# Three networks in one kernel: tiles moved to other start addresses, instructions unchanged

## The chip, the cores and the metric

The kernel runs on one core of a Trainium2 chip. The metric is the time of one execution on the device, in microseconds (us). The engines of the core are TensorE (PE, matrix products out of SBUF into PSUM), VectorE (DVE), ScalarE (ACT), GpSimd (POOL) and SyncE (SP, which issues loads and stores).

## The reference: what is computed

An attention with a sliding window and a few sink keys, then two feed-forward networks one after the other, all in float32:

```python
scores = np.where(keep, scale * (q @ k.T), -1e9)      # 2 x 8 heads x 768 x 64; keep: sink | window of 128
x = softmax(scores) @ v                               # as 1536 tokens x 512
h = x @ w_in                                          # 512 x 2048
g = where(h >= 1, h, where(h <= -1, 0, (h + 1)**2 / 4))
x = g @ w_out                                         # 2048 x 512
h = x @ w2_in
g = where(h > 0, h, exp(min(h, 0)) - 1)
out = g @ w2_out
```

The weights come as 64-bit floats and are turned into 32-bit ones on the chip.

## The kernel before

**Tiling.** Tokens lie on the free axis in three blocks of 512 (xh, xl: 128 partitions x 4 parts of the model width x 512 tokens). Each network takes the hidden width in 16 slices of 128. An item is one network, one block of 512 tokens, one slice: 2 x 3 x 16 = 96 items. For accuracy each operand of a product is split into a high part and the rest of it (xh and xl, wh and wl, gh and gl, written as fp32r by the copies and subtractions in lines 159, 161, 188 and 189), and each product is three matmuls: high x high, high x rest, rest x high.

**An item.** `gemm1` (line 172) makes h of 128 x 512 in 4 x 3 matmuls: the split first weights wh0, wl0 are stationary, the tokens xh, xl move, 512 columns in each. ScalarE and VectorE turn h into g and split it (lines 179 to 189). `gemm2` (line 211) adds the slice's part of the output to four PSUM tiles y0 to y3, again in 4 x 3 matmuls of 512 columns. In the first network the second weights wh1, wl1 are stationary and gh, gl move; in the second network gh, gl are stationary and wh1, wl1 move. The names in the trace don't carry the digit: wh in line 172 is wh0, in line 211 wh1. `finish` (line 268) does the second product of the last two items.

**Order.** `run` goes through the items: `gemm1` of item i, then `gemm2` of item i - 2. PE has this order written out, and so has GpSimd; the other engines have theirs from the program's order. In the first network `between` pulls in steps of attention: transposes of k and q with the identity idn moving (line 472), scores (509), transposes of the exponentials P, idn moving again (541), values (565), and the sinks' part, with pst moving (598, 602). Loads are issued by SyncE, some ahead of their use; conversion of the weights (lines 139 to 146) runs some units ahead of the items. There is a second path for other windows, behind a test at the end; it isn't taken here.

**Where tiles lie.** A pool takes the next free bytes of each partition, in the order in which pools are opened; a tile's start is rounded up to 32 bytes. `const` is first and holds small tiles, some of them asked for late. Then come the tokens (pool x), attention's pools (ld, v, qk, p, pt, xb, s), and the pools of `Moe` (wf, wst, wc, wsp, wso, mt, mg). nb, the row maxima of attention (asked for in line 498), is in attention's pool s.

Of the kernel before, what the change touches and what calls it, by code (L numbers as in the profile page):

```python
# [7 lines left out]
F32 = mybir.dt.float32  # L8
# [12 lines left out]
KW = BLK + NSINK  # L21
HB = BLK // 2
BW = KW + HB + NSINK
NEG = -1.0e30
FILL = -1.0e9


def f32(ap):
    return ap.bitcast(F32)


def read_params(nc, const, n_sink, window):
# [250 lines left out]
class Attn:  # L283


    def __init__(self, tc, ctx, q, k, v, xts, idn, const, segs, nq=2):
        self.tc, self.nc = tc, tc.nc
        nc = self.nc
        self.q, self.k, self.v, self.xts = q, k, v, xts
        self.B, self.H, self.S, self.D = q.shape  # L290
        self.scale = 1.0 / float(self.D) ** 0.5
        self.idn, self.const = idn, const
        self.nq = nq
        pool = lambda n, b, **kw: ctx.enter_context(tc.tile_pool(name="a_" + n, bufs=b, **kw))
        self.ld_p = pool("ld", 4)
        self.v_p = pool("v", 3)
        self.qk_p = pool("qk", 2)
        self.p_p = pool("p", 3)
        self.pt_p = pool("pt", 2)
        self.xb_p = pool("xb", 1)  # L300
        self.s_p = pool("s", 2)
        self.ps = pool("ps", 2, space=PSUM)
        self.sk, self.kept = {}, {}
        self.turn, self.spare = 0, []
        self.nat = {}
        self.first = None
        self.jobs = [(s, pr) for s in segs for pr in range(self.H // 2)]
        for what in "kq":
            self.load(what, *self.jobs[0])
# [8 lines left out]
    def masks(self, prm):  # L318
# [20 lines left out]
        for m, d, k in ((m0, far, ks), (m1, ring, kn)):  # L339
# [3 lines left out]
            nc.vector.tensor_scalar(out=m[:, sink], in0=key[:, 0:NSINK], scalar1=ns, scalar2=None, op0=ALU.is_ge)  # L343
            nc.vector.tensor_scalar(out=m, in0=m, scalar1=NEG, scalar2=None, op0=ALU.mult)
        nc.vector.tensor_scalar(out=m2[:, at], in0=ring, scalar1=w, scalar2=NEG, op0=ALU.is_ge, op1=ALU.mult)
        nc.vector.tensor_copy(m2[:, sink], m1[:, sink])
# [142 lines left out]
    def st_S(self, seg, pr, st):  # L489

        nc, D, nq = self.nc, self.D, self.nq
        b, q0 = seg[0], seg[1]
        qT, T = st["qk", pr]
        Tk = T.rearrange("p j k -> p (j k)")
        if "sm" not in st:
            st["sm"] = self.s_p.tile([128, nq, self.H], F32, tag="sm", name="sm")
            st["ps"] = self.s_p.tile([128, nq, self.H * (NSINK + 2)], F32, tag="psn", name="psn")
        nb = self.s_p.tile([128, nq, 2], F32, tag="nb", name="nb")
        P = st["P", pr] = self.p_p.tile([128, nq, 2, KW], F32, tag="P", name="P")
        S = [self.bank([128, 512], "S") for _ in range(2)]  # L500
        lead = HB + NSINK
        for n in range(nq):
            u = lead + n * BW
            for h in range(2):
                hs = slice(h * D, (h + 1) * D)
                for c in range(2):
                    o, r = (u - c * lead, n * KW + c * HB) if q0 + n else (u, KW)
                    N = (KW + (HB, lead)[c]) if q0 + n else KW
                    nc.tensor.matmul(S[h][c * HB:(c + 1) * HB, o:o + N], lhsT=qT[hs, n, c * HB:(c + 1) * HB],  # L509
                                     rhs=Tk[hs, r:r + N], start=True, stop=True, skip_group_check=True)  # L510
        n0 = 0 if q0 else 1
        for h in range(2):
            a = S[h][:, lead:lead + nq * BW].rearrange("p (n c) -> p n c", c=BW)
            lo = S[h][:, 0:nq * BW].rearrange("p (n c) -> p n c", c=BW)
            for c, to, data in ((0, a[:, :, 0:HB], a[:, :, KW:KW + HB]), (1, a[:, :, HB:BLK], lo[:, :, 0:HB])):
                r = slice(c * HB, (c + 1) * HB)
                nc.vector.copy_predicated(to[r, n0:], self.pick[r].unsqueeze(1).to_broadcast([HB, nq - n0, HB]), data[r, n0:])
            for n in range(nq):
                o = P[:, n, h, :]
                dv = nc.vector.tensor_tensor_reduce(out=o, in0=a[:, n, 0:KW], in1=self.mask[min(q0 + n, 2)], op0=ALU.add, op1=ALU.min,  # L520
                                                    scale=-self.scale, scalar=3.0e38, accum_out=nb[:, n, h:h + 1])
                ac = nc.scalar.activation(o, o, AF.Exp, bias=nb[:, n, h:h + 1], scale=-1.0,  # L522
                                          accum_out=st["sm"][:, n, 2 * pr + h:2 * pr + h + 1])
        if (seg, pr) == self.jobs[2]:
            self.first = (ac.ins, dv.ins)
# [181 lines left out]
def attention_moe_moe(ctx, tc, q, k, v, n_sink, window, w_in, w_out, w2_in, w2_out, out):  # L707
    nc = tc.nc
    B, H, S, D = q.shape
    NT, DM = out.shape  # L710
    const = ctx.enter_context(tc.tile_pool(name="const", bufs=1))
    xp = ctx.enter_context(tc.tile_pool(name="x", bufs=1))
    ws = ((w_in, w_out), (w2_in, w2_out))

# [5 lines left out]
    nc.gpsimd.affine_select(out=idn, in_=idn, pattern=[[-1, 128]], compare_op=ALU.not_equal, fill=1.0, base=0,  # L720
                            channel_multiplier=1)
    NX = NT // 512
    xts = []
    for t in range(NX):
        xts.append((xp.tile([128, DM // 128, 512], F32R, tag=f"xh{t}", name=f"xh{t}"),
                    xp.tile([128, DM // 128, 512], F32R, tag=f"xl{t}", name=f"xl{t}")))
    full = [(t, 0, 512) for t in range(NX)]

    with ExitStack() as c2:
        NQ = 2  # L730
        segs = []
        for b in range(B):
            for q0 in range(0, S // BLK, NQ):
                tok = b * S + q0 * BLK
                segs.append((b, q0, tok // 512, tok % 512))
        attn = Attn(tc, c2, q, k, v, xts, idn, const, segs, nq=NQ)
        moe = Moe(tc, c2, ws, out, xts, (full, full), half)

        attn.load("q", *attn.jobs[1])
        warm = const.tile([128, 1], F32, tag="warm", name="warm")  # L740
        nc.scalar.activation(warm, half, AF.Exp)

        zero = moe.t_p.tile([128, 512], F32, tag="g", name="zero")
        nc.vector.memset(zero, 0.0)
        bank = moe.h_ps.tile([128, 512], F32, tag="h", name="warmup")
        for _ in range(3):
            nc.tensor.matmul(bank, lhsT=zero[:, 0:128], rhs=zero, start=True, stop=True)
        prm = params(nc, const, raw)
        attn.masks(prm)
        gen = attn.stages()  # L750
        done = [0]

        def go(n=None, upto=None):

            while done[0] < len(segs) and (n is None or n > 0) and (upto is None or done[0] < upto):
                if next(gen) is not None:
                    done[0] += 1
                n = None if n is None else n - 1

        need = [(t * 512 + c0 + n) // (NQ * BLK) for t, c0, n in full] + [0]  # L760
        attn.spare = [lambda shape, name, t=t: moe.y_ps.tile(shape, F32, tag=t, name=name) for t in ("y0", "y1", "y2", "y3")]
        attn.spare += [lambda shape, name: moe.h_ps.tile(shape, F32, tag="h", name=name)] * 2

        for what, j in (("k", 1), ("k", 2), ("q", 2), ("k", 3), ("q", 3), ("v", 0)):
            attn.load(what, *attn.jobs[j])
        attn.load_vsink()
        attn.sink_sets()
        with tc.manual_schedule(engines={mybir.EngineType.PE, mybir.EngineType.Pool}):
            moe.load(1)
            attn.load("v", *attn.jobs[1])  # L770
            moe.load(3)
            go(n=18)
            flag = windowed(tc, const, prm)
            go(upto=need[0])
        moe.behind = attn.first
        attn.spare = []
        credit = [0.0]

        def between(i):
            m, tb, f = moe.items[i]  # L780
            if m == 1 or done[0] >= len(segs):
                return
            j = i // moe.KF
            credit[0] += PULLS[j]
            while credit[0] >= 1.0:
                credit[0] -= 1.0
                if done[0] < len(segs):
                    go(n=1)
            if f == moe.KF - 1 and moe.last_call:
                go(upto=need[j + 1])  # L790

        moe.run(between)
# [40 lines left out]
```

## Time and profile before

| what | us |
|---|---|
| median of three runs | 667.52 |
| the three runs | 667.35, 667.52, 668.36 |
| the profiled execution | 668.36 |
| its span, first to last instruction | 666.2 |
| PE / ACT / DVE / POOL busy in it | 631.7 / 444.2 / 386.8 / 303.7 |

The profiled execution is one of the three. Busy time of PE is the union of matmuls whose ends are modelled and which overlap: one matmul stands with 0.39 us in the trace where the next begins 0.23 us later. So the pace of PE is read from the distance of starts, or from the chain of waits, and not from the time of one matmul. The granted clock is the share of TensorE's full clock (2.4 GHz) in a stretch.

### The profile page before, as it was taken

Reading aid. Unit: us, or ns where it says so; the run is one execution under the profiler, and the core shown is the slowest. Engines: PE = TensorE matmul, PEld = TensorE weight load, DVE = VectorE, ACT = ScalarE, POOL = GpSimd, SP = SyncE. Lnnn points to the kernel's source line nnn. Section 1 sums busy time; section 2 is a strip of 40 time slices with the busy share of each in tenths; the row PEclk is TensorE's granted clock in tenths of the full one; section 3 lists DMA queues with packets and bytes.
Section 4 is the critical chain, followed back from the end, with each engine's and each line's share of the span. In section 5 each row is a group of like instructions: output and inputs, shape, how many; then the busy total and the mean of one; then the engine's idle time right before and its main releaser. Section 6 shows DMA issues by size and latency. Waiting matters only on the chain.

```text
span 666.2 us, 9583 instructions
## 1 busy us (share of the span) xinstructions
PE 631.7 (95%) x3202; PEld 489.3 (73%) x3202; DVE 386.8 (58%) x805; ACT 444.2 (67%) x922; POOL 303.7 (46%) x337
## 2 busy tenths in 40 slices
PE   6678989989999999999999999999999999999996
PEld 3446766756767777788788888888888888888884
DVE  5689999999736443425988778776432222322221
ACT  5677989788667666657688777776655555555542
POOL 4462122522354555644546555555444444444431
PEclk9798999989999999999999999999999999999999
DMA  5666455456310100001534323330010000100001
GB/s 122 161 166 191 133 171 163 139 155 175 95 29 14 24 5 9 1 0 32 157 96 125 97 95 95 95 95 32 0 64 1 1 1 0 64 0 1 1 0 69
DMA packets 66923, 47.92 MB, mean 72 GB/s; under 512 B 44848, under 2 KB 61232, under 8 KB 66864
## 3 DMA queue, kind: packets, MB, share of 16 engines
q1 hardware_dynamic: 65632, 46.96, 24.6%
q8 instruction: 27, 0.44, 0.3%
q10 hardware_dynamic: 1232, 0.26, 0.2%
q14 instruction: 32, 0.26, 0.1%
HBM read 44.06 MB, written 3.15 MB: 71 GB/s over the span
## 4 chain that ended last, share of the span: by engine, by line
PE 75%; DVE 8%; ACT 6%; DMA 4%; issue 3%; POOL 1%; SPq 1%; POOLq 0%; ACTq 0%; DVEq 0%
PE h L172 34%; PE y L211 33%; PE ops L565 2%; PE S L509 2%; DMA st<-in_moe_w_in_dram 2%; DVE ca L144 2%; DVE F L146 2%; ACT P L522 1%; PE qkps L472 1%; PE tps L541 1%; ACT F L140 1%; ACT ca L139 1%; DMA kn<-in_k_dram 1%; DVE ca L143 1%; PE y L268 1%
## 5 line engine op out<-in xcount | busy, mean ns | idle before, releaser
L161 POOL TENSOR_TENSOR wl<-F,wh 128x512 fp32r<-128x512 f32 x160 | 219.8, 1378 | 220.7 <-ACT wh L159 204.8
L159 ACT CAST wh<-F 128x512 fp32r<-128x512 f32 x192 | 117.0, 617 | 97.5 <-PE h L172 87.5
L172 PE MATMUL h<-xh,wh 128*128 128x512 f32 x384 | 154.3, 402 | 0.8 <-DVE g L181 0.5
L172 PE MATMUL h<-xl,wh 128*128 128x512 f32 x384 | 152.3, 397 | 0.9 <-POOL xl L609 0.9
L172 PE MATMUL h<-xh,wl 128*128 128x512 f32 x384 | 151.9, 395 | 0.0
L189 DVE TENSOR_TENSOR gl<-g,gh 128x512 fp32r<-128x512 f32 x96 | 72.7, 758 | 51.5 <-ACT gh L188 51.1
L185 DVE SCALAR_TENSOR_TENSOR g<-g,h 128x512 f32<-128x512 f32 x48 | 33.0, 687 | 115.4 <-ACT g L184 115.4
L188 ACT CAST gh<-g 128x512 fp32r<-128x512 f32 x96 | 59.6, 621 | 57.1 <-DVE g L185 36.1
L172 PEld LDWEIGHTS h<-xh,wh 128*128 128x128 f32 x384 | 72.0, 188 | 21.3 <-issue 3.6
L172 PEld LDWEIGHTS h<-xl,wh 128*128 128x128 f32 x384 | 72.2, 188 | 18.3 <-POOL xl L609 1.5
L172 PEld LDWEIGHTS h<-xh,wl 128*128 128x128 f32 x384 | 72.1, 188 | 17.3
L211 PE MATMUL y<-gh,wh 128*128 128x512 f32 x192 | 77.9, 406 | 0.0
L146 DVE CUSTOM_DVE_ANT_0 F<-ca,F 128x1024 uint16<-128x1024 uint16 x64 | 74.3, 1164 | 4.3 <-DVE ca L144 1.8
L211 PE MATMUL y<-gl,wh 128*128 128x512 f32 x192 | 75.4, 393 | 0.0
L211 PE MATMUL y<-gh,wl 128*128 128x512 f32 x192 | 75.4, 393 | 0.0
L211 PE MATMUL y<-wl,gh 128*128 128x512 f32 x184 | 72.1, 392 | 0.0
L211 PE MATMUL y<-wh,gh 128*128 128x512 f32 x184 | 71.8, 390 | 0.0
L211 PE MATMUL y<-wh,gl 128*128 128x512 f32 x184 | 71.6, 389 | 0.0
L181 DVE SCALAR_TENSOR_TENSOR g<-h,g 128x512 f32<-128x512 f32 x48 | 32.9, 686 | 52.0 <-ACT g L180 51.6
L547 POOL TENSOR_SCALAR_AFFINE_SELECT pt<-pt 128x512 f32<-128x512 f32 x48 | 35.7, 744 | 32.5 <-ACT pt L545 30.9
L139 ACT ACTIVATE ca<-st 128x512 f32<-128x512 f32 x64 | 43.1, 674 | 7.4 <-DVE F L146 3.4
L144 DVE SCALAR_TENSOR_TENSOR ca<-st,ca 128x512 int32<-128x512 int32 x64 | 47.3, 742 | 1.1
(111 smaller groups left out, 887.9 us busy)
## 6 DMA issues: line engine op xcount, KB each, us to landing
st<-in_moe_w_in_dram SPq DMA_DIRECT2D x32, 512.0 KB, 3.9
st<-in_moe_w_out_dram SPq DMA_DIRECT2D x32, 512.0 KB, 3.5
kn<-in_k_dram SPq DMA_DIRECT2D x48, 64.0 KB, 2.1
vn<-in_v_dram SPq DMA_DIRECT2D x32, 96.0 KB, 2.3
out_dram<-o SPq DMA_DIRECT2D x12, 256.0 KB, 2.1
qn<-in_q_dram SPq DMA_DIRECT2D x44, 64.0 KB, 2.1
vn<-in_v_dram SPq DMA_DIRECT2D x16, 64.0 KB, 3.3
qn<-in_q_dram ACTq DMA_DIRECT2D x4, 64.0 KB, 4.0
```

The lines of the kernel that those rows point to most:

```text
L139: nc.scalar.activation(a, w1.bitcast(F32), AF.Copy, scale=2.0 ** -112)
L144: nc.vector.scalar_tensor_tensor(out=ai, in0=w1, scalar=-0x80000000, in1=ai, op0=ALU.bitwise_and, op1=ALU.bitwise_or)
L146: nc.vector.tensor_tensor(out=r, in0=ai, in1=r, op=ALU.add)
L159: nc.scalar.copy(hi, src)
L161: (nc.vector if i < self.KF else nc.gpsimd).tensor_tensor(out=lo, in0=src, in1=f32(hi), op=ALU.subtract)
L172: nc.tensor.matmul(h, lhsT=w[:, k * 128:(k + 1) * 128], rhs=x[:, k, c0:c0 + n], start=(k == 0 and p == 0), stop=(k == self.KD - 1 and p == 2))
L181: nc.vector.scalar_tensor_tensor(out=g, in0=h, scalar=1.0, in1=g, op0=ALU.max, op1=ALU.min)
L185: nc.vector.scalar_tensor_tensor(out=g, in0=g, scalar=-1.0, in1=h, op0=ALU.add, op1=ALU.max)
L188: ac = nc.scalar.copy(gh, g)
L189: dv = nc.vector.tensor_tensor(out=gl, in0=g, in1=f32(gh), op=ALU.subtract)
L211: nc.tensor.matmul(self.y[c], lhsT=a, rhs=b, start=(first and p == 0), stop=(last and p == 2))
L547: nc.gpsimd.affine_select(out=o, in_=new, pattern=[[0, 2 * nq], [-sg, 128]], compare_op=op, fill=0.0, base=0, channel_multiplier=sg)
```

## The change

Three things are done to the pools. A tile that nothing writes, 32 bytes of it by `fill_to_row`, is put at the end of attention's pools, so that what comes next starts at a multiple of 256 bytes. The same is done at the end of `const`. And nb gets a pool of its own (a_nb, two buffers) behind `const`, ahead of the tokens. `CONST_END` and `ATTN_BYTES` are the bytes in use at those places. Each engine's instructions, their order, their operands apart from the addresses, and their waits are those of before.

```diff
--- before.py
+++ after.py
@@ -21,12 +21,21 @@
 KW = BLK + NSINK
 HB = BLK // 2
 BW = KW + HB + NSINK
+ROW = 256
+CONST_END = 26528 + 64
+ATTN_BYTES = 38656
 NEG = -1.0e30
 FILL = -1.0e9
 
 
 def f32(ap):
     return ap.bitcast(F32)
+
+
+def fill_to_row(pool, used):
+    n = -used % ROW
+    if n:
+        pool.tile([128, n // 4], F32, tag="fill", name="fill")
 
 
 def read_params(nc, const, n_sink, window):
@@ -300,6 +309,7 @@
         self.xb_p = pool("xb", 1)
         self.s_p = pool("s", 2)
         self.ps = pool("ps", 2, space=PSUM)
+        fill_to_row(pool("fill", 1), ATTN_BYTES)
         self.sk, self.kept = {}, {}
         self.turn, self.spare = 0, []
         self.nat = {}
@@ -495,7 +505,7 @@
         if "sm" not in st:
             st["sm"] = self.s_p.tile([128, nq, self.H], F32, tag="sm", name="sm")
             st["ps"] = self.s_p.tile([128, nq, self.H * (NSINK + 2)], F32, tag="psn", name="psn")
-        nb = self.s_p.tile([128, nq, 2], F32, tag="nb", name="nb")
+        nb = self.nb_p.tile([128, nq, 2], F32, tag="nb", name="nb")
         P = st["P", pr] = self.p_p.tile([128, nq, 2, KW], F32, tag="P", name="P")
         S = [self.bank([128, 512], "S") for _ in range(2)]
         lead = HB + NSINK
@@ -709,6 +719,7 @@
     B, H, S, D = q.shape
     NT, DM = out.shape
     const = ctx.enter_context(tc.tile_pool(name="const", bufs=1))
+    nb_p = ctx.enter_context(tc.tile_pool(name="a_nb", bufs=2))
     xp = ctx.enter_context(tc.tile_pool(name="x", bufs=1))
     ws = ((w_in, w_out), (w2_in, w2_out))
 
@@ -720,6 +731,7 @@
     nc.gpsimd.affine_select(out=idn, in_=idn, pattern=[[-1, 128]], compare_op=ALU.not_equal, fill=1.0, base=0,
                             channel_multiplier=1)
     NX = NT // 512
+    fill_to_row(const, CONST_END)
     xts = []
     for t in range(NX):
         xts.append((xp.tile([128, DM // 128, 512], F32R, tag=f"xh{t}", name=f"xh{t}"),
@@ -734,6 +746,7 @@
                 tok = b * S + q0 * BLK
                 segs.append((b, q0, tok // 512, tok % 512))
         attn = Attn(tc, c2, q, k, v, xts, idn, const, segs, nq=NQ)
+        attn.nb_p = nb_p
         moe = Moe(tc, c2, ws, out, xts, (full, full), half)
 
         attn.load("q", *attn.jobs[1])
```

Where tiles start within 256 bytes of a partition, from the built programs (several values are those of several buffers):

| tile | role | before | after |
|---|---|---|---|
| xh, xl | moving in line 172 | 160 | 0 |
| wh0, wl0 | stationary in line 172 | 224 | 0 |
| gh, gl | moving, then stationary in line 211 | 224 | 0 |
| wh1, wl1 | stationary, then moving in line 211 | 224 | 0 |
| st, F, ca, g | weights as loaded and converted, gate | 224 | 0 |
| kn, qn, vn | attention's loads | 160 | 0 |
| idn | moving in transposes | 192 | 192 |
| qkT | transposed k and q | 160, 0 | 0, 96 |
| P | exponentials | 96, 160, 224 | 192, 0, 64 |
| pt, pst, xb | transposed P, sinks, attention's output | 32 | 128 |
| vs, one | stationary beside pst | 160 | 192 |

Slices of 128 or 512 columns within these tiles lie at multiples of 512 bytes from their starts.

## Rows read from the trace of the kernel before

**Rows 1.** The page, part 1: engine, busy us, share of the span, instructions.
```profile
PE 631.7 (95%) x3202; PEld 489.3 (73%) x3202; DVE 386.8 (58%) x805; ACT 444.2 (67%) x922; POOL 303.7 (46%) x337
```

**Rows 2.** Busy us of each engine by stage, (x) instructions, granted clock, DMA share.
```profile
core 0: us, PE busy (x) PEld busy (x) DVE busy (x) ACT busy (x) POOL busy (x), PEclk, DMA share, GB/s
0.00:60.00 60.00, 41.84 (x348) 26.43 (x348) 41.85 (x172) 41.93 (x128) 32.07 (x90) 0.89 0.63 156
60.00:166.00 106.00, 97.87 (x556) 71.45 (x556) 100.01 (x242) 90.40 (x208) 27.75 (x45) 0.98 0.55 158
166.00:276.40 110.40, 108.91 (x646) 81.52 (x645) 55.91 (x146) 72.21 (x171) 55.92 (x67) 1.00 0.11 28
276.40:648.10 371.70, 371.46 (x1610) 301.22 (x1609) 185.57 (x244) 235.24 (x411) 185.41 (x135) 1.00 0.15 47
```

**Rows 3.** The chain that ended last, us 490 to 512: start, us, what.
```profile
498.69 2.80 PE h L172 x12
501.49 2.74 PE y L211 x12
```

**Rows 4.** PE's matmuls by line, from 276.4, from 166 and from 60 us.
```profile
L172 PE MATMUL h<-xh,wh 128*128 128x512 f32 x268 | 105.7, 394 | 0.2 <-DVE g L181 0.2
...
L211 PE MATMUL y<-wl,gh 128*128 128x512 f32 x180 | 70.6, 392 | 0.0
...
L211 PE MATMUL y<-gl,wh 128*128 128x512 f32 x88 | 34.5, 392 | 0.0
...
L211 PE MATMUL y<-gh,wh 128*128 128x512 f32 x58 | 24.2, 418 | 0.0
L172 PE MATMUL h<-xh,wh 128*128 128x512 f32 x57 | 24.0, 421 | 0.0
...
L172 PE MATMUL h<-xh,wh 128*128 128x512 f32 x55 | 23.0, 419 | 0.3 <-DVE g L181 0.3
...
L211 PE MATMUL y<-gh,wh 128*128 128x512 f32 x47 | 19.8, 421 | 0.0
```

**Rows 5.** PE's waits before 60 us: us in total, times, longest.
```profile
PE qkps L472 <- DMA kn<-in_k_dram: 6.8, 1, 6.8
PE tps L541 <- ACT P L522: 4.3, 5, 1.8
```

**Rows 6.** PE in order of time, one pass: start us, us, what.
```profile
498.53 0.39 PE L172 MATMUL h<-xh,wh 128*128 128x512 f32 x1
...
501.33 0.39 PE L211 MATMUL y<-wh,gh 128*128 128x512 f32 x1
...
502.71 0.39 PE L211 MATMUL y<-wh,gh 128*128 128x512 f32 x1
...
504.07 0.39 PE L172 MATMUL h<-xh,wh 128*128 128x512 f32 x1
```

**Rows 7.** The weight loads in the same pass (same columns).
```profile
498.54 0.19 PEld L172 LDWEIGHTS h<-xl,wh 128*128 128x128 f32 x1
...
501.33 0.19 PEld L211 LDWEIGHTS y<-wl,gh 128*128 128x128 f32 x1
```

**Rows 8.** PE in attention, from 34.7 us: start us, us, what, count.
```profile
34.81 0.38 PE L472 MATMUL qkps<-idn,kn 128*128 128x128 f32 x2
35.03 0.38 PE L472 MATMUL qkps<-idn,qn 128*128 128x128 f32 x2
...
38.32 0.40 PE L602 MATMUL rps<-pst,one 112*128 112x256 f32 x2
38.56 0.40 PE L598 MATMUL xps<-pst,vs 112*128 112x256 f32 x2
38.79 0.40 PE L602 MATMUL rps<-pst,one 112*128 112x256 f32 x2
```

**Rows 9.** ScalarE in the same pass as rows 6.
```profile
501.88 0.59 ACT L183 ACTIVATE g<-h 128x512 f32<-128x512 f32 x1
```

**Rows 10.** The page, part 6: issues, KB each, median us to landing.
```profile
kn<-in_k_dram SPq DMA_DIRECT2D x48, 64.0 KB, 2.1
```

## The prediction

> **What bounds the kernel now.** I read the busy line first: TensorE (PE) is busy for 631.7 of 666.2 us, no other engine for more than 444.2 [rows 1]. Such a share is a mean, so I cut the span into stages. From 276.4 to 648.1 us PE is busy for 371.46 of 371.70 us, at a granted clock of 1.00 (the 2.4 GHz level), while VectorE, ScalarE and GpSimd have 186, 235 and 185 us of work [rows 2]. The chain of waits says the same: 12 matmuls of line 172, then 12 of line 211, without end and with no other engine between them, 2.80 and 2.74 us each [rows 3]. Line 172 multiplies the tokens (moving xh, xl) by the split first weights, line 211 the gated part by the second weights. One pass of 24 matmuls takes 2.80 + 2.74 = 5.54 us, and there are 67 of them: three groups of 268 matmuls of line 172 in that stage, and of line 211 three of 180 (second network) and three of 88 (first), the first of each in [rows 4].
>
> Before that, PE is busy for 108.91 of 110.40 us from 166 to 276.4, and nearly all of it is on the chain again. From 60 to 166 us PE has 97.87 of 106 us and VectorE 100.01: VectorE bounds as much as PE. Before 60 us neither does alone (41.8 us each) [rows 2]; there PE waits 6.8 us for a load of k and 4.3 us for ScalarE's exponentials [rows 5].
>
> **The pace of one matmul.** Twelve matmuls of line 172 in 2.80 us are 233.3 ns each. The last six of a line 211 block go from 502.71 to the next block at 504.07: 1.36 us, 226.7 ns each; its first six take 1.38 us [rows 6]. A matmul of 512 columns at one column a cycle of 2.4 GHz is 512 / 2.4 = 213.3 ns. So a matmul of line 172 loses 20.0 ns and one of line 211 13.4 ns, though shape, type, clock and number of instructions are the same, and nobody is waited for. What differs? The moving operand of line 172 starts at byte 160 of a 256-byte row; that of line 211 at byte 224, in the first network (gh, gl) as in the second (wh1, wl1). The stationary operand starts at 224 in both lines. Its load cannot make the difference either: it begins within 0.01 us of the matmul before and takes 0.19 us in both lines [rows 6, 7]. So I read the two paces as the price of where the moving operand starts.
>
> What an operand at the start of a 256-byte row costs, this trace does not show for this kind of matmul. Bounds: below, 213.3 ns, which the clock sets; above, the 226.7 and 233.3 ns of today. The nearest row with a moving operand at a multiple of 64 bytes is that of the transposes: idn, at 192, moves in them. Two take 0.22 us, 110 ns each for 128 columns, which is two cycles a column (106.7 ns) and some 3 ns [rows 8]. They read at half the rate and so may hide a loss, but they show that little is lost between two matmuls as such. The products with pst moving (256 columns, start at 32) are the counter-case at full rate: 0.23 and 0.24 us for two, 115 to 120 ns where the clock allows 106.7, a loss of 8 to 13 ns on half as many columns, much like line 172's [rows 8]. I take 213.3 + 3 = 216 ns, the value nearest to the transposes.
>
> The Trainium skill (TensorE: Matmul & The Clock Gate, section "Wait — 56ns, not 53.3ns?") gives 215.7 ns from start to start for 512 columns at the full clock, without a word on where operands start. No matmul of 512 columns here reaches that; by it the sum below would be 30.4 us instead of 29.7.
>
> **The change part by part.** No instruction is added, taken away or moved, no wait and no DMA; the fillers are never written. What changes is where tiles start.
>
> Tokens, split weights and gated parts go from 160 and 224 to 0. A pass of 24 becomes 24 x 216 = 5.184 us. I leave the 0.02 us by which the first six of a line 211 block are slower (ScalarE reads h out of PSUM from 501.88 to 502.47 [rows 9]), so 5.204: 0.336 us gained per pass, 14.0 ns a matmul. Stage by stage:
> - 276.4 to 648.1 us: 67 passes x 0.336 = 22.5 us, all on the path. Who would be late next? The busiest other engine, ScalarE, has 235 us for what would be 349 [rows 2].
> - 166 to 276.4 us: 169 matmuls of line 172 (57 + 56 + 56) and 174 of line 211 (3 x 58; the first group of each in [rows 4]), 343 x 14.0 = 4.8 us, on the path since PE idles 1.5 us there.
> - 60 to 166 us: 167 (55 + 56 + 56) and 139 (47 + 46 + 46) = 306 matmuls [rows 4], 4.3 us. VectorE has only 6 us of slack there, and part of it is spent waiting for PE; I take half, 2.1 us, and keep nothing and 4.3 as ends.
> - after 648.1 us: 24 matmuls of line 268 (two last parts x 4 column blocks x 3), 0.3 us.
> Sum 29.7 us.
>
> Loads (kn, qn, vn, st) land at 0 instead of 160 or 224. Before 60 us this could touch the wait of 6.8 us for kn; from nothing to 6.8 either way. I take nothing: kn's median landing is 2.1 us [rows 10], so that wait is a queue of loads, not the slowness of one.
>
> Attention's own tiles only swap odd starts for odd starts: qkT from 160 and 0 to 0 and 96, P from 96, 160, 224 to 192, 0, 64, pt and pst from 32 to 128. Their matmuls are 250 + 303 = 553 in the two middle stages (556 - 306 and 646 - 343 [rows 2, 4]); most are fp32 products, which read no faster than the transposes. Nothing, with 553 x 3 ns = 1.7 us as the end either way. VectorE, ScalarE and GpSimd work on the same tiles; if their instructions change, they have a third of the long stage or more to hide it in [rows 2].
>
> Profiled run 668.4 - 29.7 = 638.7 us; the median of the three runs is 0.8 us under the profiled one, so 638 us.
>
> **The rivals.**
> *Part of the loss is not the start's.* The 13.4 ns of line 211 may be the price of changing stationary operands, with only the 6.7 ns between the lines due to the start (or to moving and stationary operand starting differently: 160 against 224 in line 172, 224 against 224 in line 211; after the change they agree everywhere). Then line 172 falls to 226.7 and line 211 stays: 6.7 ns x (804 + 169 + half of 167) = 7.1 us, 660 us. For: line 211's two halves of a network, with other operands moving, have one and the same loss. Against: the transposes change their stationary operand each time too and lose 3 ns. Between this and the forecast lies all from 645 to 664.
>
> *Starts do nothing.* The two paces could belong to something else that differs between the lines, such as 12 matmuls into one PSUM bank against 3. Against: inside its three, line 211 still goes at 226.7. Time: 667.5.
>
> The Trainium skill (SBUF — State Buffer, section "Specifications (TRN2)") speaks against this change: it counts in lines of 16 bytes, and 160, 224 and 0 are all multiples of 16, so by it all paces would be alike and the time would stay. Rows 6 disagree: 233.3 against 226.7 ns.
>
> *The row's start is the worst place: slower.* Two points allow another line: the pace falls by 6.7 ns as the start rises by 64 bytes, and jumps back at the block's end. With blocks of 128 bytes, 160 and 224 are 32 and 96, and 0 gives 236.7 ns: 12 x 3.3 + 12 x 10 = 160 ns more per pass, 10.7 us in the long stage and some 3.3 before, 681 us. With blocks of 256 bytes it gives 250 ns: 0.46 us a pass, 708 us. For: pst at 32 pays what 160 pays, as blocks of 128 say. Against: with blocks of 256 pst should take 123 ns, and it takes 115 to 120; and nothing in a read that begins at a boundary explains more work than one that straddles it. It decides as soon as the common pace is over 230.8 ns.
>
> **How the numbers follow.** Forecast (628 to 645 us): 0.55. Part of the loss only (645 to 664): 0.22. No change: 0.10. Slower: 0.13. The low end is the clock's: 17.5 ns x 2,281 matmuls = 39.9 us, 628. To leave out no more than 2 in 10 the range must take in no change: 628 to 668. A measurement can tell some 0.2% (1.3 us): faster 0.77, same 0.10, slower 0.13.
>
> **What would show it.** Right: in the long stage both lines' matmuls start 0.216 us apart, the chain's pieces of 12 are 2.60 us each and a pass 5.20 us, with the same counts of instructions. If line 172 alone falls to 0.227, the first rival holds; if both stay at 2.80 and 2.74, the second; if both stand at one pace over 0.231, the third. If the long stage gains 22 us and the stretch from 60 to 166 us nothing, VectorE took it. It is wrong if the gain lies before 60 us, in loads.

## The result, and the profile after

The changed kernel takes 662.06 us (median of 4 runs, 659.93 to 662.74) against 667.94 us for the kernel before (4 runs, 667.35 to 668.46). The ratio is 0.9907, with a 95% interval of 0.9882 to 0.9931: faster by some 0.9%, 5.9 us. The forecast was 638 us. A second set of runs of the same kernel (e7 below) gave 0.988 (0.9852 to 0.9908). The sign was right; the size was a fifth of what was forecast, and the time is that of the first rival.

One thing is not as the section on the change has it. `fill_to_row` puts 32 bytes behind `const`, but nothing behind attention's pools: without nb they take 38,656 bytes, which is already a multiple of 256. So what brought the networks' pools to 0 is that nb left attention's pools.

The profiled execution took 662.16 us, its span is 660.0 us. First the page's busy line, to be held against [rows 1], then the stages (columns as in [rows 2]), then the chain of waits as in [rows 3]. Line 181 is now the first product (172 before), line 220 the second (211 before).

```profile
PE 623.8 (95%) x3202; PEld 489.7 (74%) x3202; DVE 386.0 (58%) x805; ACT 445.1 (67%) x922; POOL 305.1 (46%) x337
```

```profile
60.80:168.30 107.50, 97.77 (x563) 72.05 (x564) 102.08 (x246) 92.56 (x212) 27.79 (x46) 1.00 0.56 159
168.30:276.20 107.90, 106.69 (x639) 80.27 (x638) 53.68 (x143) 70.95 (x169) 56.98 (x67) 1.00 0.10 26
276.20:641.70 365.50, 365.03 (x1610) 301.62 (x1609) 185.53 (x244) 235.47 (x411) 186.22 (x135) 1.00 0.15 48
```

```profile
495.03 2.72 PE h L181 x12
497.75 2.72 PE y L220 x12
```

The same 1610 matmuls of the long stage take 365.5 us instead of the 371.7 of [rows 2]: that is 6.2 us, the whole difference of the spans (666.2 - 660.0). Both products now run at 2.72 us for 12, which is 226.7 ns a matmul: the first product came down from 233.3, and the second stayed at its settled pace. The other engines have the same work as before. The first 276 us gained 0.2 us.

PE in order of time, one block of the second product and the start of the next block (columns as in [rows 6]):

```profile
503.02 0.39 PE L220 MATMUL y<-wh,gh 128*128 128x512 f32 x1
...
504.38 0.39 PE L220 MATMUL y<-wh,gh 128*128 128x512 f32 x1
...
505.74 0.39 PE L181 MATMUL h<-xh,wh 128*128 128x512 f32 x1
```

The first six of the block take 1.36 us like the last six. Before, they took 1.38 [rows 6].

### The profile page after: what moved, and what is told of

It is laid out like the page before. It is cut to its first block, busy times and chain, and to the rows that moved or that the text cites. A ratio compares the mean times of both kernels' runs of the same rounds, so it can differ in the third digit from the quotient of the medians.

```text
span 660.0 us, 9583 instructions
## 1 busy us (share of the span) xinstructions
PE 623.8 (95%) x3202; PEld 489.7 (74%) x3202; DVE 386.0 (58%) x805; ACT 445.1 (67%) x922; POOL 305.1 (46%) x337
## 4 chain that ended last, share of the span: by engine, by line
PE 80%; ACT 5%; DVE 5%; DMA 4%; issue 3%; POOL 1%; POOLq 0%; DVEq 0%; ACTq 0%; SPq 0%
PE h L181 35%; PE y L220 34%; PE ops L575 3%; PE S L519 2%; DMA st<-in_moe_w_out_dram 2%; PE qkps L482 2%; DMA st<-in_moe_w_in_dram 2%; PE tps L551 1%; ACT P L532 1%; DVE ca L153 1%; DMA kn<-in_k_dram 1%; DVE F L155 1%; PE warmup L760 1%; ACT F L149 1%; PE y L277 1%
## 5 line engine op out<-in xcount | busy, mean ns | idle before, releaser
L170 POOL TENSOR_TENSOR wl<-F,wh 128x512 fp32r<-128x512 f32 x160 | 220.6, 1386 | 213.3 <-ACT wh L168 196.3
L181 PE MATMUL h<-xh,wh 128*128 128x512 f32 x384 | 152.5, 398 | 1.5 <-DVE g L190 0.9
L181 PE MATMUL h<-xl,wh 128*128 128x512 f32 x384 | 150.3, 391 | 0.9 <-POOL xl L619 0.9
L181 PE MATMUL h<-xh,wl 128*128 128x512 f32 x384 | 150.0, 391 | 0.0
L557 POOL TENSOR_SCALAR_AFFINE_SELECT pt<-pt 128x512 f32<-128x512 f32 x48 | 37.3, 777 | 31.5 <-ACT pt L555 29.8
```

What stands on the lines that cost most here:

```text
L170: (nc.vector if i < self.KF else nc.gpsimd).tensor_tensor(out=lo, in0=src, in1=f32(hi), op=ALU.subtract)
L181: nc.tensor.matmul(h, lhsT=w[:, k * 128:(k + 1) * 128], rhs=x[:, k, c0:c0 + n], start=(k == 0 and p == 0), stop=(k == self.KD - 1 and p == 2))
L557: nc.gpsimd.affine_select(out=o, in_=new, pattern=[[0, 2 * nq], [-sg, 128]], compare_op=op, fill=0.0, base=0, channel_multiplier=sg)
```

## The experiments

All kernels that compute the networks have the same instructions in the same order; only unused tiles, which push others along, and the place of nb differ. Times are medians, ratios are to runs of the kernel before on the same chip.

**e1: what does a matmul cost, by the starts of its two operands?** The disputed cost can be measured by itself. The core of the kernel (REP is 16):

```python
for a in range(8):                   # moving operand at 32 * a bytes (ma ... mh)
    for b in range(8):               # stationary operand at 32 * b bytes (sa ... sh)
        h = ps.tile([128, 512], F32, tag="h", name="h")
        for j in range(REP):
            nc.tensor.matmul(h, lhsT=s[b], rhs=m[a], start=(j == 0), stop=(j == REP - 1))
```

> This kernel computes none of the networks; its output is a part of q. It runs fp32r matmuls of 512 columns back to back, 16 of a kind, with the moving operand (ma to mh) and the stationary one (sa to sh) each starting 0, 32, ... 224 bytes into a 256-byte row, 64 kinds; then some with fewer columns, narrower stationary operands, and bfloat16 ones. Theory A, the moving operand's start alone sets the pace: a kind with mf (160) takes 233.3 ns a matmul and kinds with ma (0) and mh (224) 226.7, whatever the stationary one's start. Theory B, the distance between the two starts sets it: the eight kinds with equal starts take 226.7 and the kind mf, sh 233.3. Theory C, the two paces have nothing to do with starts: all 64 alike. On the rest of the loss, 226.7 against 213.3: if it is the weight load's, narrower stationary operands or bfloat16 ones come nearer to 213.3; if it is a share of the columns, 256 columns lose 6.7 ns, if it is fixed, 13.4.

PE in order of time; each row is the 16 matmuls of one kind, and the distance to the next row's start, divided by 16, is nearly its pace:

```profile
19.26 3.80 PE L48 MATMUL h<-ma,sa 128*128 128x512 f32 x16
22.90 3.89 PE L48 MATMUL h<-ma,sb 128*128 128x512 f32 x16
26.62 3.90 PE L48 MATMUL h<-ma,sc 128*128 128x512 f32 x16
30.36 3.90 PE L48 MATMUL h<-ma,sd 128*128 128x512 f32 x16
34.09 3.88 PE L48 MATMUL h<-ma,se 128*128 128x512 f32 x16
37.81 3.90 PE L48 MATMUL h<-ma,sf 128*128 128x512 f32 x16
41.55 3.84 PE L48 MATMUL h<-ma,sg 128*128 128x512 f32 x16
45.22 3.89 PE L48 MATMUL h<-ma,sh 128*128 128x512 f32 x16
...
186.35 3.80 PE L48 MATMUL h<-mf,sf 128*128 128x512 f32 x16
189.98 3.89 PE L48 MATMUL h<-mf,sg 128*128 128x512 f32 x16
...
253.17 3.80 PE L48 MATMUL h<-mh,sh 128*128 128x512 f32 x16
```

Taken from the starts of the third to the sixteenth matmul of each kind (the first ones still settle), and put in order by the distance from the moving operand's start to the stationary one's, modulo 256 bytes, eight kinds to a distance:

| distance, bytes | 0 | 32 | 64 | 96 | 128 | 160 | 192 | 224 |
|---|---|---|---|---|---|---|---|---|
| mean, ns | 226.9 | 233.3 | 233.5 | 234.3 | 232.7 | 233.2 | 229.1 | 233.2 |
| lowest and highest | 226.6, 228.6 | 232.5, 233.5 | 233.4, 233.5 | 234.0, 234.4 | 232.5, 233.7 | 233.1, 233.6 | 229.1, 229.2 | 233.1, 233.5 |

The distance decides: all eight equal starts, from 0 to 224, settle at 226.7 ns (one of them, mb with sb, needs seven matmuls to settle there, hence 228.6), and each other distance has one price, within 1.3 ns, wherever the moving operand starts. Theory A (the moving operand's start) falls, theory B (the distance) stands. The kernel before has 160 and 224 in the first product, a distance of 64: 233.5 in the table, 233.3 in [rows 6].

The last rows of this kernel are on what is left, the 13.4 ns over 213.3:

```profile
256.80 2.95 PE L53 MATMUL h<-ma,sa 128*128 128x384 f32 x16
...
265.22 2.07 PE L53 MATMUL h<-ma,sa 128*128 128x256 f32 x16
267.12 1.98 PE L53 MATMUL h<-mf,sh 128*128 128x256 f32 x16
268.94 2.06 PE L53 MATMUL h<-ma,se 128*128 128x256 f32 x16
...
276.15 3.84 PE L53 MATMUL h<-ma,sa 128*64 128x512 f32 x16
279.82 3.89 PE L53 MATMUL h<-mf,sh 128*64 128x512 f32 x16
...
287.23 3.86 PE L53 MATMUL h<-ma,sa 128*32 128x512 f32 x16
290.93 3.87 PE L53 MATMUL h<-mf,sh 128*32 128x512 f32 x16
...
298.35 3.63 PE L57 MATMUL h<-xa,ya 128*128 128x512 bf16 x16
301.81 3.62 PE L57 MATMUL h<-xc,ya 128*128 128x512 bf16 x16
305.26 3.62 PE L57 MATMUL h<-xc,yg 128*128 128x512 bf16 x16
308.72 3.62 PE L57 MATMUL h<-xa,yg 128*128 128x512 bf16 x16
```

With bfloat16 operands 16 matmuls of 512 columns take 3.45 us (301.81 to 305.26), by the starts of the single ones 215.8 to 215.9 ns each, and the four pairs of starts tried (moving at 0 or 32 bytes, stationary at 0 or 96) make no difference. So the remaining loss belongs to fp32r; whether to its products or to its weight loads, which stand with 0.19 us in the trace and those of bfloat16 with 0.10, isn't shown. With equal starts it doesn't shrink with the columns: 256 columns take 119.5 ns where the clock allows 106.7, 12.8 more. There the order is even the other way round: the kind mf, sh, a distance of 64, takes 113.3 ns (1.82 us for 16 in the rows), so equal starts are the best of the table for 512 columns, not for all widths. A stationary operand of 64 or 32 columns instead of 128 doesn't make matmuls of 512 columns faster but a little slower (3.67 and 3.70 us for 16 of them with equal starts, 229 and 231 ns), and there other starts cost at most 3 ns more.

**e2 to e4: one half of the change alone, and equal starts that are no multiples of 256.** The edits, in this order, are a filler in the changed kernel (tokens at 0, networks' pools at 224), and one in the kernel before (tokens at 160, pools at 0, then pools at 160):

```diff
-        fill_to_row(pool("fill", 1), ATTN_BYTES)
+        pool("fill", 1).tile([128, 56], F32, tag="fill", name="fill")
...
+        pool("fill", 1).tile([128, 8], F32, tag="fill", name="fill")
...
+        pool("fill", 1).tile([128, 48], F32, tag="fill", name="fill")
```

> Tokens and all before them start as in the changed kernel (0), the pools of the networks as in the kernel before (224). Theory A (the moving operand's start alone): line of the first product 2.72 us for 12 and the second 2.72 to 2.74, about 661 to 662 us, the whole gain. Theory B (distance between the two operands): the first product has 0 against 224, a distance it has in neither kernel, so it stays slow, about 2.80, and the second is fast: 667 us. Theory C (starts do nothing, the change of time is elsewhere): any time between.

> Tokens start as in the kernel before (160), the pools of the networks at 0. Theory A: the first product still moves an operand at 160: 2.80 us for 12, second 2.72 to 2.74, about 667 us, no gain. Theory B: 160 against 0 is unequal, first product slow, second product fast: 667 us too.

> Tokens as in the kernel before (160), the pools of the networks at 160 too, so all operands start alike, but at no multiple of 64. Theory A: both products move operands at 160: 2.80 us each for 12, a pass of 24 in 5.60 instead of 5.54, about 672 us. Theory B: equal starts everywhere, 2.72 us each for 12, 661 us.

| | distance, first product | second | time, us | ratio (95%) |
|---|---|---|---|---|
| before | 64 | 0 | 668.38 | 1 |
| e2, tokens only | 224 | 0 | 668.08 | 0.9998 (0.9978 to 1.0018) |
| e3, networks only | 96 | 0 | 667.47 | 0.9993 (0.9979 to 1.0007) |
| e4, all at 160 | 0 | 0 | 660.18 | 0.9890 (0.9863 to 0.9917) |

The chain of waits in the long stage of e2, e3 and e4 (start, us, what):

```profile
494.93 2.80 PE h L181 x12
497.74 2.76 PE y L220 x12
```

```profile
497.22 2.73 PE y L211 x12
499.95 2.81 PE h L172 x12
```

```profile
497.12 2.72 PE y L211 x12
499.84 2.72 PE h L172 x12
```

Each half of the change alone is worth nothing, and e4 has the whole gain with no operand of the networks at a multiple of 64 bytes. In the first product even the small differences are those of the table: 234.3 ns at distance 96 makes 2.81 for 12, where 224 makes 2.80. One piece was foreseen by no theory: the second product of e2 has equal starts and takes 2.76, not 2.72 to 2.74; e9 comes back to that. It isn't 256 bytes that count, but that both operands start alike.

**e5: finer steps.** The same kind of kernel, with the moving operand at 0 and the stationary one in steps of 4 bytes, then kinds in turn and other widths.

> This kernel computes none of the networks; its output is a part of q. The moving operand starts at 0 (maa), the stationary one in steps of 4 bytes from 0 to 252 (saa, sab, ... shh), 12 matmuls of each. If whole units of 32 bytes decide, the first eight kinds all take 226.7 ns; if the equality must be exact, only saa does. If 226.7 is not the floor, some start in between goes below it. Then pairs: matmuls that alternate between two kinds. The load of a weight runs beside the matmul ahead of it. If it is this neighbour that counts, (0,0) and (96,96) in turn are slow, near 233, and (0,96) and (96,0) in turn, unequal in themselves, are fast, near 227; if the two operands of one matmul count, the reverse. Last, fewer columns with equal and unequal starts: a loss per matmul stays near 13 ns from 512 down to 320 columns, a loss per column shrinks with them.

Some of its rows in order of time, 12 matmuls each (saa is 0, sab 4, sac 8; sdb is 100, sdc 104):

```profile
20.60 2.89 PE L46 MATMUL h<-maa,saa 128*128 128x512 f32 x12
23.33 2.94 PE L46 MATMUL h<-maa,sab 128*128 128x512 f32 x12
26.11 2.93 PE L46 MATMUL h<-maa,sac 128*128 128x512 f32 x12
...
90.40 2.89 PE L46 MATMUL h<-maa,sdb 128*128 128x512 f32 x12
93.12 2.96 PE L46 MATMUL h<-maa,sdc 128*128 128x512 f32 x12
```

Four bytes off are enough (2.78 us to the next row instead of 2.73), so no unit of 32 bytes is shared. But sdb, at 100 bytes, goes at 226.7 too, as do 120, 144, 156, 228 and 252 among others. Equality is sufficient for 512 columns, as far as tried, and not necessary. No kind of 512 columns settles under 226.7 ns: that is a floor. With equal starts 320 columns take 146.9 ns (133.3 by the clock), 13.6 more, the loss of 512 columns; at 448 and 480 it is 16 and 18, and there the distance of 64 is 1 to 2 ns better. Narrow ones stop falling: 192 and 128 columns both take 112 ns. The kinds in turn were slow in both patterns (234 ns, and 230 as 236 and 224 in turn), which answers the question of the neighbour only by half; e10 takes it up.

**e6: the mirror.** If the distance is the cause, it can be put where it wasn't:

```diff
+        pool("gap", 1).tile([128, 24], F32, tag="gap", name="gap")
         self.g_p = pool("mg", LAG + 1)
```

> The changed kernel with one filler of 96 bytes ahead of the gated parts gh and gl: tokens and weights start at 0, gh and gl at 96. If the distance of the two operands sets the pace, the first product stays at 2.72 us for 12 and the second becomes slow in both networks, 2.80 to 2.81: a pass of 5.52 to 5.53 instead of 5.44, about 668 us. If starts other than those of the tokens don't matter, 662 us.

667.51 us, ratio 0.9993 (0.9977 to 1.0009). The chain (the first product is line 182, the second 221):

```profile
495.88 2.81 PE y L221 x12
498.69 2.73 PE h L182 x12
```

The second product is now the slow one, and the gain is gone. Theory B called both numbers.

**e7 and e8: is a multiple of 256 worth something of its own?** The changed kernel and the kernel of e4, on one chip.

> The changed kernel itself, on the same chip as the next run. Theory B (equal starts) gives it the same time as the next, 660 to 662 us; if multiples of 256 bytes are worth something of their own, in loads or attention, it is faster than the next.

> The kernel before with the networks' pools moved to 160, as in e4. Theory B: equal to the run ahead of it within 0.3%.

659.66 us, 0.988 (0.9852 to 0.9908), and 661.40 us, 0.9912 (0.9891 to 0.9932). The intervals overlap, and in e4 the order was the other way round (660.18 there). No worth of 256 bytes is to be seen.

**e9: a distance of 192, which costs little in the table.** The kernel before with a filler of 128 bytes, which puts the networks' pools at 96:

> The kernel before with the networks' pools at 96, so the stationary operand of the first product starts 64 bytes below the moving one (160), and the second product's two are equal (96). The table of 64 kinds gives 229.1 ns for that distance and 226.7 for equal starts. Theory B (distance): 12 matmuls of the first product in 2.75 us, of the second in 2.72 to 2.75, a pass of 5.48 to 5.50, about 663 to 664 us, between the kernel before and the changed one. If only equality counts and all unequal starts are alike: 2.80 and 2.73, 667 us.

666.99 us, 0.9988 (0.9973 to 1.0002): a miss by 3 us. That the rival of the last sentence named 667 is luck: its pieces were to be 2.80 and 2.73.

```profile
500.84 2.77 PE y L211 x12
503.61 2.76 PE h L172 x12
```

The first product does what the table says, 2.76 for 12 where 229.1 ns make 2.75. The second, with equal starts, takes 2.77 instead of 2.72. One block shows why: from start to start its twelve take 234, 231, 233, 236, 224, 231, 236, 228, 232, 231, 227 and 227 ns. It comes down to 226.7 only after ten. The first and the eleventh of them (columns as in [rows 6]), 2.32 us apart where ten at 226.7 ns make 2.27:

```profile
500.68 0.40 PE L211 MATMUL y<-wh,gh 128*128 128x512 f32 x1
...
503.00 0.39 PE L211 MATMUL y<-wl,gh 128*128 128x512 f32 x1
```

A pace once disturbed takes some matmuls to come to rest, and here the block of 12 is nearly over by then. In e2 it takes six, at 224 to 236 ns, which makes its 2.76; in [rows 6] this is the 1.38 us of the first six. Why it takes ten behind a distance of 192 and fewer behind others, no run here shows.

**e10: whose start counts?** Two kinds of matmul in turn, at 0 and at a shift. In "own" each has equal starts, in "next" the weight that is loaded beside it starts where its moving operand does.

> This kernel computes none of the networks; its output is a part of q. Two kinds of matmul in turn, 40 of each row, for a shift of 0, 32, ... 224 bytes (a to h). In rows 'own' each matmul has equal starts (0,0 then shift,shift), so the weight that is loaded beside it, its neighbour's, starts elsewhere. In rows 'next' each matmul is unequal in itself (moving 0 with stationary at the shift, then the reverse), but the weight loaded beside it starts where its moving operand does. If the weight load beside a running matmul is what collides with it, all 'next' rows take 226.7 ns and the 'own' rows 229 to 234 but for a. If a matmul's own two operands count, the reverse. Rows of both sorts in between would say that both count.

PE in order of time, 40 matmuls to a row (a: shift 0, d: 96; each time the next row's start stands below):

```profile
25.10 9.23 PE L42 MATMUL own<-ma,sa 128*128 128x512 f32 x40
34.17 9.23 PE L45 MATMUL next<-ma,sa 128*128 128x512 f32 x40
43.23 9.45 PE L42 MATMUL own<-mb,sb 128*128 128x512 f32 x40
...
80.26 9.55 PE L42 MATMUL own<-md,sd 128*128 128x512 f32 x40
89.64 9.37 PE L45 MATMUL next<-md,sd 128*128 128x512 f32 x40
98.85 9.31 PE L42 MATMUL own<-me,se 128*128 128x512 f32 x40
```

From a row's start to the next one's, divided by 40: 226.7 for both rows of a; 234.5 and 230.2 for d. Over all shifts but that of a "own" rows take 228.8 to 234.5 and "next" rows 230.0 to 233.3 ns. Neither sort alone is enough. Whatever meets, it is more than a pair: of the shifts tried here, only 0, with all operands of the stretch starting alike, stays at the floor.

## Why the prediction was wrong, point by point

- **What bounds the kernel** was right: the long stage is PE's, and its gain is the whole gain of the span.
- **The pace of one matmul.** That starts set the two paces was right, and e4 and e6 show it. Which starts, was wrong: I ruled out the stationary operand because its load has the same time and the same start in both lines [rows 7], and read 160 and 224 as two prices of the moving operand. Equal starts in the second product (224, 224) were the reason that it was fast, so it had nothing left to gain but its settling. The reading "160 against 224, and 224 against 224" stood in the first rival's brackets; it is the one that holds.
- **The failed term is the 216 ns.** It was taken from the transposes (110 ns for 128 columns, [rows 8]), read as two cycles a column and some 3 ns of loss. But in e1 fp32r matmuls of 128 columns take 111.7 ns too, at each of the three pairs of starts tried: a pace near 110 ns at that width says nothing of the loss at 512 columns. The floor of an fp32r matmul of 512 columns is 226.7 ns in all of e1, e5 and e10: 13.4 ns over the clock's 213.3, wherever the equal starts lie. 24 x 226.7 = 5.44 us a pass, not 5.184; 0.100 us gained and not 0.336, and 67 x 0.100 = 6.7 us, of which the long stage shows 6.2. The value between the bounds that I should have weighed more is the one that needed no new pace, since the second product already had it.
- **The 0.02 us in the first six** of a block I put down to ScalarE reading h [rows 9]. ScalarE still reads h there (from 503.58 us in the same block), and the 0.02 is gone. It was the settling after an unequal block, which e9 shows at its largest.
- **The figure of the Trainium skill** (TensorE: Matmul & The Clock Gate, section "Wait — 56ns, not 53.3ns?"), 215.7 ns for 512 columns, is confirmed by e1's bfloat16 rows with 215.9. It doesn't hold for fp32r, and I had put it beside a sum for fp32r.
- **From 60 to 166 us** half of the gain was to stay, and the profiles can't tell. From the first item to 168.3 us the stage took 107.5 us (59.4 to 167.4, 108.0 us, before): 0.5 of some 1.3 us. But the clock differs. From 136 to 139 us the granted clock of the kernel before is 0.50 (the 1.2 GHz level), soon after 2.0 us in which PE did nothing; in the changed kernel PE does nothing for 2.1 us at the same place, and the clock stays. From 135 to 140 us (columns as in [rows 2]), before and after:

```profile
135.00:140.00 5.00, 4.52 (x19) 2.98 (x20) 4.31 (x15) 4.27 (x15) 2.26 (x5) 0.66 0.52 139
```

```profile
135.00:140.00 5.00, 2.80 (x18) 1.91 (x18) 4.84 (x18) 4.29 (x14) 0.78 (x2) 1.00 0.45 136
```

  The profiles of e2, e3, e4, e6 and e9 have such a fall too, those of e7 and e8 have none, though e8 is the kernel of e4. Over the stage's 306 matmuls of the networks, with attention's work between them, the four profiles with equal starts take 104.5 to 107.3 us and that of the kernel before 106.5: they differ by more than the term. So what VectorE kept isn't shown. From there to 276.2 us the gain is 1.1 us.
- **Before 60 us** I took nothing, with 1.7 us of attention either way. The first item starts at 60.83 us after and 59.36 before. In the profiles with attention's tiles where the change puts them it starts at 59.72 to 60.83 (four), in those with the old places at 58.86 to 59.78 (five): perhaps 0.8 us lost to attention's starts. It isn't settled; the clock's rise at the start also differs from run to run (granted clock 0.86 to 0.89 before 60 us, in both sorts).
- **The rivals.** "Part of the loss is not the start's" gave 660 us with 6.7 ns x 1,057 matmuls, and 660 to 662 was measured. Its cause, a price of changing stationary operands, is not shown: the 13.4 ns stay, but bfloat16 matmuls that load a weight each lose only 2.6 ns, and fp32r ones with narrower weights, loaded in 0.13 us instead of 0.19, lose no less. "The row's start is the worst place" falls with e1's first row of the table: 0 is as good as any. "Starts do nothing" falls with e4.
- **The rule of 16-byte lines** (the Trainium skill, SBUF — State Buffer, section "Specifications (TRN2)") would make all these starts alike; e1 shows 226.7 to 234.3 ns among starts that are all multiples of 32.

## What to carry to other kernels

Where fp32r matmuls of 512 columns and 128 stationary columns follow one another with a weight load each, let all their operands, moving and stationary, start at the same place modulo 256 bytes; which place, doesn't matter (all eight multiples of 32 in e1, and 0 and 160 in the kernel itself), and for other widths the table has to be measured. Half of it was worth nothing here: one operand group that starts elsewhere costs up to 7.6 ns in each of its own matmuls (at multiples of 32 bytes) and disturbs up to ten of the next ones. And a bound for an unseen pace should come from an instruction of the same type and width: the row of 128 columns couldn't show the loss that 512 columns have.

## What was not expected of the hardware

- An fp32r matmul of 512 columns, with its weight load, goes at 226.7 ns at best where bfloat16 goes at 215.9, at the same clock. With equal starts the loss is 13 to 18 ns at each width tried from 256 to 512 columns. At 192 and 128 columns there is another floor, 112 ns. What makes either, no run here shows.
- The distance in bytes between moving and stationary operand changes the pace, with one price for each distance from 32 to 224 bytes in steps of 32 at 512 columns, and another order at 256. Between these steps single distances (100, 120, 144 bytes and others) go at the floor too. The Trainium skill (TensorE: Matmul & The Clock Gate, section "Step-by-step: what each phase is for") says that loading the next weights takes no read bandwidth from the running matmul. e1 and e10 speak against that for fp32r: the start of the loaded operand alone moves the pace by up to 7.6 ns (226.7 to 234.3 in the table). That the two streams of reads collide is the nearest explanation, and an argued one: no view of the profile shows a read.
- The disturbed paces aren't noise but patterns that repeat (236 and 224 ns in turn, or 231, 238, 231), and equal starts come to rest only after up to ten matmuls.
